# One slot plan for the LayerNorm steps of both attention halves

## The chip, the cores and the metric

The kernel runs on one core of a Trainium2 chip. The metric is device time in microseconds (us) of one execution. Engines are named as in the profile: PE (TensorE matmuls), PEld (its weight loads), DVE (VectorE), ACT (ScalarE), POOL (GpSimd), SP (SyncE, which here only issues DMAs). Every engine takes its instructions in the order in which they stand in its own queue.

## The reference

One transformer block on x of 2048 rows by 512, with modulation by a conditioning vector c. Attention has 32 query heads in groups of 4 per key/value head (8 of these, 128 wide) over the last 512 keys of a cache; the feed-forward network (FFN) is a gated GELU of width 1792.

```python
mod = (_silu(c) @ w_mod).reshape(c.shape[0], 6, 1, -1)
sa, ca, ga, sb, cb, gb = (mod[:, j] for j in range(6))
h = _layernorm(x) * (1 + ca) + sa
q = h @ wq                                   # 32 heads of 128
p = softmax(q @ k^T * Dh ** -0.5)            # k, v: last 512 rows of the caches
x = x + ga * ((p @ v) @ wo)
h = _layernorm(x) * (1 + cb) + sb
x = x + gb * ((gelu(h @ w_gate) * (h @ w_up)) @ w_down)
```

## The kernel before

Matrix products are made of three fp16 matmuls each (`mm3`, lines 86 to 88): every operand is held as a high half and a low half, and high x high, high x low and low x high are added up in PSUM. Rows of x are handled in four blocks of 512 (QB). Attention runs over two halves of the rows, each half two blocks; for each half it goes through 16 pairs of heads, and for each pair through 4 units (one head, one block of 512 rows). A unit is four **slots** of 128 rows. So there are 512 slots, 16 to a pair of heads, and T = 512. In the text the place of a slot is its number modulo 16.

The order of all work is written out by a loop over slots, and no scheduler changes it. In slot t the code issues, in this order:

```python
scores(t)                      # PE: 3 matmuls into ps (2 banks)
peak(t)                        # DVE L906: nm, the negated maximum of a row
if t % 2 == 0: recips(t - 2)   # DVE L925
run(("d", t))                  # what was set down for slot t: q and PV results (L674 ACT, L675 DVE), sums (L694), y (L883)
low(t - 3)                     # DVE L934: the low half of p; then SP's transpose pt<-p (L938)
expo(t)                        # ACT L915: ee = exp(ps - max)
high(t - 2)                    # ACT L929: the high half of p
for _ in range(3): pop()       # PE: 3 groups of 3 matmuls from the queue of work
run(t); run(("w", t))          # transposes that are due; then steps placed "w": weights (POOL), LayerNorm
spare(t)                       # one of the loads and stores that may go out (bg), by their due slots
```

A slot thus has 12 matmuls, 2.59 us when PE never stops; at place 3 the queue of work is empty after 6, and the slot takes 1.3. Since ps has two banks, the scores of slot t + 2 wait until the exponential of slot t has read its bank. On DVE every slot has the maximum and the low half of p. At places 1, 3, 7, 13 and 15 that is all but for an instruction on a column now and then; at the other places there are one to three more instructions over 128x512.

During the first attention half the second half's rows of the first LayerNorm are made (`ln_pair`, gen 1), and during the second half those of the second LayerNorm for the FFN's first half (gen 2). A third run of such work, gen 3, lies under the FFN and has a plan of its own. For each gen there are four chunks (i = 0 to 3), each with two blocks of 128 rows (k = 0 and 1, tiles xs, of which there are two). Its steps are: `load` (SP: xs<-in_x or xs<-y), `stat` (DVE L381, L383, L385, and POOL's power L391), `norm` first (DVE L473: subtract the mean, times a row) and second (DVE L471: times rs, plus a row), `sub` (POOL L479, four differences, for a product with fewer multiplications), and for four sides `high` (ACT L489), `low` (POOL L492) and `turn` (SP L496, a DMA transpose into the tiles B, C, T1, T2 that PE reads).

`plan_pair` places these steps: PLAN has offsets from a base slot b, for block 0 (load, stat, norm first, norm second), for block 1 the same, then the two slots of subtractions, then (high, low, turn) of each side. Loads have due slots from b + l to b + l + 3. With the numbers before, gen 1 has b = 78 + 32 i and gen 2 b = 287 + 48 i.

Beside LayerNorm POOL prepares weights in the first half: scales (kmax, lw, vmax and so on: a power L233, then L237), wq by L160, L156, L157, L729, and wo by L584, L156, L157. DVE takes reciprocals of these scales (kinv L248, wsc L271, lr L263, vsc L648) in its own queue three slots after the scale was set down. In the second half POOL prepares the FFN's weights (stage), which SP stores (kept<-stage).

Of the kernel before, what the change touches and what calls it, by code (L numbers as in the profile page):

```python
# [25 lines left out]
QT = QB // P  # L26
# [37 lines left out]
def block_kernel(ctx: ExitStack, tc: tile.TileContext, x, kT, v, wq, wo, wg, wu, wd, cT, wc, wm, out):  # L64
# [35 lines left out]
    def rows_of(t, i):  # L100
        return t[i * P:(i + 1) * P, :]
# [233 lines left out]
    def within(lo, hi, fn):  # L335
        at(("w", max(lo, 0)), lambda: bg.append((hi, lo, 0, fn)))
# [6 lines left out]
    BK, hs, y1 = {}, {}, {}  # L343
# [113 lines left out]
    def ln_pair(gen, i, src):  # L457
        by, shift = (1, 0) if gen < 2 else (4, 3)
        X, S, st = {}, {}, [{}, {}]

        def load(k):
            X[k] = pool.tile([P, D], F32, tag="ln", name="xs", bufs=2)
            dma(X[k], src(k))

        def stat(k):
            ln_stat(X[k], st[k])
            ln_power(st[k])

        def norm(k, second):
            if second:  # L470
                nc.vector.scalar_tensor_tensor(X[k], X[k], st[k]["rs"], ROWS[shift], op0=ALU.mult, op1=ALU.add)  # L471
            else:
                nc.vector.scalar_tensor_tensor(X[k], X[k], st[k]["mv"][:, 0:1], ROWS[by], op0=ALU.subtract, op1=ALU.mult)  # L473

        def sub(o, a, b):
            def at_(n):
                return X[n // 2][:, n % 2 * 256:n % 2 * 256 + 256]

            nc.gpsimd.tensor_tensor(at_(o), at_(a), at_(b), op=ALU.subtract)  # L479

        def alloc(s):
            S[s] = pool.tile([P, 1 if s == 1 else 2, 2, 256], F16, tag="turn", name="turn", bufs=2)

        def side(s):
            k = (0, 1, 0, 1)[s]
            return X[k][:, 256:512].rearrange("p (h q) -> p h q", h=1) if s == 1 else X[k].rearrange("p (h q) -> p h q", h=2)

        def high(s):
            nc.scalar.activation(S[s][:, :, 0, :], side(s), AF.Copy)  # L489

        def low(s):
            nc.gpsimd.tensor_tensor(S[s][:, :, 1, :], side(s), S[s][:, :, 0, :], op=ALU.subtract)  # L492

        def turn(s):
            moved[0] += 1
            nc.sync.dma_start_transpose(block(gen, ("B", "C", "T1", "T2")[s])[:, i], S[s].rearrange("p a b c -> p (a b c)"))  # L496

        return load, stat, norm, sub, alloc, high, low, turn
# [167 lines left out]
    def at(key, *fns):  # L666
        later.setdefault(key, []).extend(fns)
# [259 lines left out]
    def high(t):  # L927
        p16 = pool.tile([P, 2, W], F16, tag="p16", name="p16", bufs=NP16)
        nc.scalar.activation(p16[:, 0, :], E[t]["e"], AF.Copy, scale=E[t]["r"])  # L929
        E[t]["p16"] = p16  # L930

    def low(t):
        p16 = E[t]["p16"]
        nc.vector.scalar_tensor_tensor(p16[:, 1, :], E[t]["e"], E[t]["r"], p16[:, 0, :], op0=ALU.mult, op1=ALU.subtract)  # L934
        u, i = divmod(t, 4)
        if i == 0:
            pT[u] = pool.tile([P, QT, 2 * KT, P], F16, tag="pt", name="pt", bufs=NPT)
        nc.sync.dma_start_transpose(pT[u][:, i], p16.rearrange("p a b -> p (a b)"))  # L938
        E.pop(t)
# [158 lines left out]
    for p in range(2):  # L1098
        for k, (load, steps) in enumerate(combos(p, nc.gpsimd if p == 0 else nc.vector, 1 if p else 2, 0 if p else 5)):
# [5 lines left out]
            else:  # L1105
                sched(base + steps[0][0], (load, [fn for _, fn in steps]), *[base + off for off, _ in steps[1:]])

    PLAN = {1: (-6, 0, 2, 4, -1, 6, 8, 16, 20, 21, ((8, 9, 12), (18, 19, 22), (24, 25, 28), (28, 29, 33))),
            2: (-6, 0, 2, 5, 8, 14, 16, 18, 21, 22, ((7, 8, 11), (19, 20, 23), (25, 26, 29), (31, 32, 35)))}

    def plan_pair(gen, b, i, src):
        load, stat, norm, sub, alloc, high, low, turn = ln_pair(gen, i, src)
        l0, s0, a0, b0, l1, s1, a1, b1, u, v, sides = PLAN[gen]
        for k, (l, s, x, y) in enumerate(((l0, s0, a0, b0), (l1, s1, a1, b1))):
            within(b + l, b + l + 3, lambda k=k: load(k))
            at(("w", b + s), lambda k=k: stat(k))
            at(("w", b + x), lambda k=k: norm(k, False))
            at(("w", b + y), lambda k=k: norm(k, True))
        for s, (h, l, t) in enumerate(sides):
            at(("w", b + h), lambda s=s: alloc(s), lambda s=s: high(s))  # L1120
            at(("w", b + l), lambda s=s: low(s))
            at(b + t, lambda s=s: turn(s))
        at(("w", b + u), lambda: sub(0, 2, 0), lambda: sub(2, 3, 2))
        at(("w", b + v), lambda: sub(3, 3, 0), lambda: sub(1, 1, 3))
# [3 lines left out]
    for j in (3, 4):  # L1128
        at(257 + 2 * j, lambda j=j: row_make(j))
    for i in range(QT):  # L1130
        plan_pair(1, 78 + 32 * i, i, lambda k, i=i: rows_of(x, 2 * QT + QT * k + i))
        plan_pair(2, 287 + 48 * i, i, lambda k, i=i: y1[QT * k + i])

    def store_set(key, k):
        store(("w", key, k), SET[key][k])
# [294 lines left out]
    with tc.manual_schedule():  # L1430
        begin()
        nexty = []
        for t in range(T + TAIL):
            now[0] = t
            u, s = divmod(t, 4)
# [149 lines left out]
```

## Time and profile before

| | |
|---|---|
| runs | 1762.35, 1762.66, 1764.65 us (median 1762.66) |
| the profiled execution | 1763.88 us, of which 1762.1 is the span from first to last instruction |
| granted PE clock | 0.999 |
| attention, first half | about 25 to 690 us of the span |
| attention, second half | to 1336 us |
| FFN | the rest |
| maximum (L906), alone | 0.68 us a row, 512 of them |
| low half of p (L934), median and longest | 0.74 and 1.78 us, 512 of them |

Rows of single instructions read: start (us from the span's start), duration, engine, line, operation, output<-inputs, shapes, how many; in brackets the idle time of the engine ahead of it and what ended it. A row's start is what counts for the queue, since an instruction's row may end some hundredths after the next one began. Rows of stretches read: the stretch, its length, busy time of each engine with its number of instructions, clock, DMA share, GB/s. Rows of waits read: who waited <- for whom: us in total, times, longest.

### The profile page before, as it was taken

Reading aid. Unit: us, or ns where it says so; the run is one execution under the profiler, and the core shown is the slowest. Engines: PE = TensorE matmul, PEld = TensorE weight load, DVE = VectorE, ACT = ScalarE, POOL = GpSimd, SP = SyncE. Lnnn points to the kernel's source line nnn. Section 1 sums busy time; section 2 is a strip of 40 time slices with the busy share of each in tenths; the row PEclk is TensorE's granted clock in tenths of the full one; section 3 lists DMA queues with packets and bytes.
Section 4 is the critical chain, followed back from the end, with each engine's and each line's share of the span. In section 5 each row is a group of like instructions: output and inputs, shape, how many; then the busy total and the mean of one; then the engine's idle time right before and its main releaser. Section 6 shows DMA issues by size and latency. Waiting matters only on the chain.

```text
span 1762.1 us, 25746 instructions
## 1 busy us (share of the span) xinstructions
PE 1724.3 (98%) x8034; PEld 787.8 (45%) x8034; DVE 1455.9 (83%) x2541; ACT 1207.7 (69%) x2716; POOL 896.2 (51%) x1113
## 2 busy tenths in 40 slices
PE   8899999999999999999999999999999999999999
PEld 5444444444444444444444444444444444444444
DVE  7888898989898889888888897988875788676666
ACT  6888877777777877778878778788774344434333
POOL 4879878887888773216666667666300233000000
PEclk9999999999999999999999999999999999999999
DMA  7999999999998998999999999999976545252222
GB/s 233 215 195 212 207 213 202 220 199 220 209 213 195 225 203 163 204 214 218 220 214 220 233 223 206 227 224 216 201 143 140 168 127 134 81 200 75 87 75 75
DMA packets 691690, 328.14 MB, mean 186 GB/s; under 512 B 596960, under 2 KB 607456, under 8 KB 691552
## 3 DMA queue, kind: packets, MB, share of 16 engines
q1 hardware_dynamic: 691264, 325.97, 81.0%
q8 instruction: 63, 1.03, 0.2%
q14 instruction: 75, 0.61, 0.1%
q10 hardware_dynamic: 288, 0.52, 0.1%
HBM read 127.54 MB, written 53.61 MB: 103 GB/s over the span
## 4 chain that ended last, share of the span: by engine, by line
PE 77%; POOL 8%; DVE 7%; ACT 4%; issue 2%; DMA 1%; SPq 0%; POOLq 0%; ACTq 0%
PE py L88 8%; PE py L86 8%; PE py L87 8%; PE ps L86 5%; PE ps L88 5%; PE ps L87 5%; PE po L86 5%; PE po L88 5%; PE po L87 5%; PE fa L86 3%; PE fa L88 3%; PE fa L87 3%; PE qa L86 2%; PE qa L88 2%; PE qa L87 2%
## 5 line engine op out<-in xcount | busy, mean ns | idle before, releaser
L915 ACT ACTIVATE ee<-ps,nm 128x512 f32<-128x512 f32 x512 | 350.1, 684 | 265.5 <-DVE nm L906 263.6
L934 DVE SCALAR_TENSOR_TENSOR p<-ee,rr,p 128x512 f16<-128x512 f32 x512 | 452.8, 884 | 1.8 <-ACT p L929 1.5
L906 DVE TENSOR_REDUCE nm<-ps 128x1 f32<-128x512 f32 x512 | 349.9, 683 | 97.3 <-PE ps L88 95.1
L929 ACT ACTIVATE p<-ee,rr 128x512 f16<-128x512 f32 x512 | 363.1, 709 | 8.8 <-DMA pt<-p 8.0
L86 PE MATMUL ps<-k,qt 128*128 128x512 f16 x512 | 193.8, 379 | 20.9 <-ACT ee L915 20.2
L86 PE MATMUL po<-pt,v 128*128 128x512 f16 x512 | 194.1, 379 | 1.6 <-DVE p L934 0.8
L88 PE MATMUL ps<-k,qt 128*128 128x512 f16 x512 | 194.1, 379 | 1.3 <-DVE qt L675 1.3
L87 PE MATMUL py<-wo,ot 128*128 128x512 f16 x512 | 194.0, 379 | 0.0
L88 PE MATMUL py<-wo,ot 128*128 128x512 f16 x512 | 194.0, 379 | 0.0
L88 PE MATMUL po<-pt,v 128*128 128x512 f16 x512 | 194.0, 379 | 0.0
L87 PE MATMUL po<-pt,v 128*128 128x512 f16 x512 | 194.0, 379 | 0.0
L86 PE MATMUL py<-wo,ot 128*128 128x512 f16 x512 | 194.0, 379 | 0.0
L87 PE MATMUL ps<-k,qt 128*128 128x512 f16 x512 | 193.9, 379 | 0.0
L391 POOL TENSOR_TENSOR rs<-rs,nhalf 128x1 f32<-128x1 f32 x32 | 23.4, 731 | 227.4 <-DVE rs L385 224.6
L675 DVE SCALAR_TENSOR_TENSOR ot<-po,ot 128x512 f16<-128x512 f32 x128 | 87.0, 680 | 39.5 <-ACT ot L674 39.3
L87 PEld LDWEIGHTS <-w 128*128 128x128 f16 x728 | 71.3, 98 | 87.0 <-issue 1.7
L88 PEld LDWEIGHTS <-w 128*128 128x128 f16 x728 | 71.3, 98 | 86.6 <-issue 0.8
L86 PEld LDWEIGHTS <-w 128*128 128x128 f16 x728 | 71.2, 98 | 86.7 <-DMA w<-kept 1.3
L883 DVE SCALAR_TENSOR_TENSOR acc<-py,ysc,acc 128x512 f32<-128x512 f32 x128 | 94.5, 738 | 10.9 <-PE py L88 10.9
L883 DVE SCALAR_TENSOR_TENSOR acc<-py,dysc,acc 128x512 f32<-128x512 f32 x112 | 81.3, 744 | 26.4 <-PE py L88 26.2
L915 ACT ACTIVATION_READ_ACCUMULATOR ee<-ps,nm 128x1 f32 x512 | 99.4, 194 | 0.0
L86 PE MATMUL py<-wo,at 128*128 128x512 f16 x224 | 84.9, 379 | 0.0
(269 smaller groups left out, 3760.6 us busy)
## 6 DMA issues: line engine op xcount, KB each, us to landing
w<-kept SPq DMA_DIRECT2D x123, 256.0 KB, 3.3
wo<-kept SPq DMA_DIRECT2D x60, 256.0 KB, 3.5
raw<-in_wo SPq DMA_DIRECT2D x56, 256.0 KB, 3.1
kept<-stage SPq DMA_DIRECT2D x56, 256.0 KB, 3.1
kept<-w SPq DMA_DIRECT2D x39, 256.0 KB, 3.2
rw<-in_wq SPq DMA_DIRECT2D x38, 256.0 KB, 3.2
pt<-p SPq DMA_TRANSPOSE x512, 3.4
kept<-wo SPq DMA_DIRECT2D x32, 256.0 KB, 2.7
```

The lines of the kernel that those rows point to most:

```text
L86: nc.tensor.matmul(ps, lhi, rhi, start=first, stop=False, skip_group_check=chain)
L87: nc.tensor.matmul(ps, lhi, rlo, start=False, stop=False, skip_group_check=chain)
L88: nc.tensor.matmul(ps, llo, rhi, start=False, stop=last, skip_group_check=chain)
L391: nc.gpsimd.tensor_tensor(st["rs"], st["rs"], nhalf, op=ALU.pow)
L675: return lambda: nc.vector.scalar_tensor_tensor(t[:, 1, :], src, scale, t[:, 0, :], op0=ALU.mult, op1=ALU.subtract)
L883: nc.vector.scalar_tensor_tensor(acc[ti], st["p"], by, acc[ti], op0=ALU.mult, op1=ALU.add)
L906: nc.vector.tensor_reduce(nm, E[t]["ps"], axis=AX.X, op=ALU.max, negate=True)
L915: nc.scalar.activation(e, E[t]["ps"], AF.Exp, bias=E[t]["nm"], scale=1.0, accum_out=sm[:, t % 2:t % 2 + 1])
L929: nc.scalar.activation(p16[:, 0, :], E[t]["e"], AF.Copy, scale=E[t]["r"])
L934: nc.vector.scalar_tensor_tensor(p16[:, 1, :], E[t]["e"], E[t]["r"], p16[:, 0, :], op0=ALU.mult, op1=ALU.subtract)
```

## The change

The two plans become one, and the bases move: gen 1 from 78 to 77 + 32 i, gen 2 from 287 to 285 + 48 i (both are place 13 of 16 with the new base).

```diff
-    PLAN = {1: (-6, 0, 2, 4, -1, 6, 8, 16, 20, 21, ((8, 9, 12), (18, 19, 22), (24, 25, 28), (28, 29, 33))),
-            2: (-6, 0, 2, 5, 8, 14, 16, 18, 21, 22, ((7, 8, 11), (19, 20, 23), (25, 26, 29), (31, 32, 35)))}
+    PLAN = (-6, 0, 2, 4, 0, 6, 10, 16, 19, 20, ((7, 8, 12), (17, 18, 22), (23, 24, 28), (27, 28, 32)))
...
-        l0, s0, a0, b0, l1, s1, a1, b1, u, v, sides = PLAN[gen]
+        l0, s0, a0, b0, l1, s1, a1, b1, u, v, sides = PLAN
...
-        plan_pair(1, 78 + 32 * i, i, lambda k, i=i: rows_of(x, 2 * QT + QT * k + i))
-        plan_pair(2, 287 + 48 * i, i, lambda k, i=i: y1[QT * k + i])
+        plan_pair(1, 77 + 32 * i, i, lambda k, i=i: rows_of(x, 2 * QT + QT * k + i))
+        plan_pair(2, 285 + 48 * i, i, lambda k, i=i: y1[QT * k + i])
```

As slots (chunk i = 0; the place modulo 16 in brackets):

| step | gen 1 before | gen 1 after | gen 2 before | gen 2 after |
|---|---|---|---|---|
| statistic, block 0 | 78 (14) | 77 (13) | 287 (15) | 285 (13) |
| norm first, block 0 | 80 (0) | 79 (15) | 289 (1) | 287 (15) |
| norm second, block 0 | 82 (2) | 81 (1) | 292 (4) | 289 (1) |
| load due, block 1 | 77 to 80 | 77 to 80 | 295 to 298 | 285 to 288 |
| statistic, block 1 | 84 (4) | 83 (3) | 301 (13) | 291 (3) |
| norm first, block 1 | 86 (6) | 87 (7) | 303 (15) | 295 (7) |
| norm second, block 1 | 94 (14) | 93 (13) | 305 (1) | 301 (13) |
| subtractions | 98, 99 | 96, 97 | 308, 309 | 304, 305 |
| high halves (ACT) | 86, 96, 102, 106 | 84, 94, 100, 104 | 294, 306, 312, 318 | 292, 302, 308, 312 |
| low halves (POOL) | 87, 97, 103, 107 | 85, 95, 101, 105 | 295, 307, 313, 319 | 293, 303, 309, 313 |
| transposes (SP) | 90, 100, 106, 111 | 89, 99, 105, 109 | 298, 310, 316, 322 | 297, 307, 313, 317 |

On DVE, the queue around slots 86 and 87 (gen 1, i = 0; nm is the maximum, p the low half, xs the LayerNorm tile, row the modulation row, qt and ot results of PE, acc the sum of y). Before:

```order
L906 TENSOR_REDUCE nm<-ps 128x1
L925 RECIPROCAL rr<-rr 128x2
L675 SCALAR_TENSOR_TENSOR qt<-qd,qsc,qt 128x512
L883 SCALAR_TENSOR_TENSOR acc<-py,ysc,acc 128x512
L934 SCALAR_TENSOR_TENSOR p_3158<-ee,rr,p_3158 128x512
L473 SCALAR_TENSOR_TENSOR xs<-xs,mv,row 128x512
L906 TENSOR_REDUCE nm<-ps 128x1
L934 SCALAR_TENSOR_TENSOR p_3186<-ee,rr,p_3186 128x512
L231 TENSOR_REDUCE ysc<-pst 128x1
```

The same place after the change:

```order
L906 TENSOR_REDUCE nm<-ps 128x1
L925 RECIPROCAL rr<-rr 128x2
L675 SCALAR_TENSOR_TENSOR qt<-qd,qsc,qt 128x512
L883 SCALAR_TENSOR_TENSOR acc<-py,ysc,acc 128x512
L934 SCALAR_TENSOR_TENSOR p_3160<-ee,rr,p_3160 128x512
L906 TENSOR_REDUCE nm<-ps 128x1
L934 SCALAR_TENSOR_TENSOR p_3189<-ee,rr,p_3189 128x512
L473 SCALAR_TENSOR_TENSOR xs<-xs,mv,row 128x512
L231 TENSOR_REDUCE ysc<-pst 128x1
```

The first norm step of block 1 went from the end of slot 86 to the end of slot 87.

On DVE, slots 82 to 84 (places 2 to 4) before:

```order
L883 SCALAR_TENSOR_TENSOR acc<-py,ysc,acc 128x512
L934 SCALAR_TENSOR_TENSOR p_3025<-ee,rr,p_3025 128x512
L471 SCALAR_TENSOR_TENSOR xs<-xs,rs,row 128x512
L906 TENSOR_REDUCE nm<-ps 128x1
L934 SCALAR_TENSOR_TENSOR p_3060<-ee,rr,p_3060 128x512
L906 TENSOR_REDUCE nm<-ps 128x1
L925 RECIPROCAL rr<-rr 128x2
L675 SCALAR_TENSOR_TENSOR ot<-po,ot 128x512
L934 SCALAR_TENSOR_TENSOR p_3092<-ee,rr,p_3092 128x512
L381 BN_STATS bn<-xs 128x6
```

and after:

```order
L883 SCALAR_TENSOR_TENSOR acc<-py,ysc,acc 128x512
L934 SCALAR_TENSOR_TENSOR p_3025<-ee,rr,p_3025 128x512
L906 TENSOR_REDUCE nm<-ps 128x1
L934 SCALAR_TENSOR_TENSOR p_3061<-ee,rr,p_3061 128x512
L381 BN_STATS bn<-xs 128x6
L383 BN_AGGR mv<-bn 128x2
L385 TENSOR_SCALAR rs<-mv 128x1
L906 TENSOR_REDUCE nm<-ps 128x1
L925 RECIPROCAL rr<-rr 128x2
L675 SCALAR_TENSOR_TENSOR ot<-po,ot 128x512
```

The second norm step of block 0 left slot 82, and the statistic of block 1 went from slot 84 into the short slot 83.

On POOL, slots 95 to 98 of chunk 0 (turn is a low half, xs<-xs the subtractions, lw to ksc the scales of the next pair's weights, rw the weights themselves) before:

```order
L233 TENSOR_TENSOR lw<-lw,half__86 128x1
L237 TENSOR_SCALAR lw<-lw 128x1
L237 TENSOR_SCALAR lu<-lw,kmax,ma 128x1
L259 TENSOR_TENSOR lt<-lu,half__86 128x1
L237 TENSOR_SCALAR lt<-lt 128x1
L492 TENSOR_TENSOR turn<-xs,turn 128x256
L237 TENSOR_SCALAR qsc<-lt 128x1
L237 TENSOR_SCALAR lr<-lr,lu 128x1
L237 TENSOR_SCALAR ksc<-lr,kinv 128x1
L479 TENSOR_TENSOR xs<-xs 128x256 x2
L160 TENSOR_SCALAR rw<-rw,wsc 128x512
```

and after:

```order
L492 TENSOR_TENSOR turn<-xs,turn 128x256
L233 TENSOR_TENSOR lw<-lw,half__86 128x1
L237 TENSOR_SCALAR lw<-lw 128x1
L237 TENSOR_SCALAR lu<-lw,kmax,ma 128x1
L259 TENSOR_TENSOR lt<-lu,half__86 128x1
L237 TENSOR_SCALAR lt<-lt 128x1
L479 TENSOR_TENSOR xs<-xs 128x256 x4
L237 TENSOR_SCALAR qsc<-lt 128x1
L237 TENSOR_SCALAR lr<-lr,lu 128x1
L237 TENSOR_SCALAR ksc<-lr,kinv 128x1
L160 TENSOR_SCALAR rw<-rw,wsc 128x512
```

The low half now stands ahead of the power of lw, and all four subtractions ahead of qsc, lr and ksc; before, two of them stood behind ksc and two behind the first piece of wq.

## The prediction

> **What bounds the kernel now.** I read the busy shares first, then who waited for whom on TensorE (PE) by stage, then busy time per stretch of 32 slots, and last the single rows around the stops.
>
> ```profile
> PE 1724.3 (98%) x8034; PEld 787.8 (45%) x8034; DVE 1455.9 (83%) x2541; ACT 1207.7 (69%) x2716; POOL 896.2 (51%) x1113
> ```
> ```profile
> core 0: us, PE busy (x) PEld busy (x) DVE busy (x) ACT busy (x) POOL busy (x), PEclk, DMA share, GB/s
> 571.70:652.48 80.78, 80.53 (x377) 36.44 (x376) 67.76 (x122) 63.15 (x151) 60.01 (x75) 1.00 1.00 217
> 139.75:221.04 81.29, 81.29 (x387) 37.45 (x386) 70.16 (x123) 65.56 (x156) 70.55 (x88) 1.00 0.98 210
> 252.69:337.56 84.87, 81.23 (x378) 36.46 (x378) 74.33 (x133) 65.68 (x159) 69.23 (x88) 1.00 0.94 210
> ...
> 422.38:507.20 84.82, 81.23 (x377) 36.48 (x377) 74.31 (x133) 65.69 (x159) 69.19 (x88) 1.00 0.93 209
> 507.20:591.15 83.95, 81.06 (x378) 36.29 (x377) 71.18 (x127) 67.19 (x163) 67.39 (x90) 1.00 0.93 208
> ```
> PE is the bound, at full clock, so only its stops can be won. Each stretch above is 32 slots. The first two lie before and after the LayerNorm (LN) work of the first attention half and run without a stop (one of 0.4 us in the first): 81 us. The next three (first and last shown; the middle one also takes 84.82) carry one chunk of LN each and take 84.8 with the same matmuls. Two views of waits, PE from 228 to 570 us, then from 570 to 1340 us:
>
> ```profile
> PE ps L86 <- ACT ee L915: 13.9, 15, 1.9
> PE ps L88 <- DVE qt L675: 1.0, 1, 1.0
> PE qa L86 <- ACT u L816: 0.4, 1, 0.4
> ...
> PE po L86 <- DVE p L934: 0.8, 1, 0.8
> PE ps L86 <- ACT ee L915: 0.3, 1, 0.3
> ```
> So first-half LN costs at most about 18.6 us: 15.3 us in 17 stops; 2.7 because each stop is 0.16 longer than it shows (a matmul's row lasts 0.38 us, while the next may start 0.22 after it); and some 0.6 in gaps too small for this view. In the second half there is next to nothing to win, and the third group of LN, under the FFN, is not touched. These are the stops of one chunk in order of time, then two of the last chunk:
>
> ```profile
> 252.69 0.38 PE L86 MATMUL ps<-k,qt 128*128 128x512 f16 x1 [1.63 <-ACT ee L915]
> 293.54 0.38 PE L86 MATMUL ps<-k,qt 128*128 128x512 f16 x1 [0.49 <-ACT ee L915]
> 321.27 0.38 PE L86 MATMUL ps<-k,qt 128*128 128x512 f16 x1 [0.17 <-ACT ee L915]
> 325.08 0.38 PE L86 MATMUL ps<-k,qt 128*128 128x512 f16 x1 [1.06 <-ACT ee L915]
> 337.56 0.38 PE L86 MATMUL ps<-k,qt 128*128 128x512 f16 x1 [1.91 <-ACT ee L915]
> ...
> 538.65 0.38 PE L86 MATMUL ps<-k,qt 128*128 128x512 f16 x1 [0.85 <-ACT ee L915]
> 550.93 0.38 PE L86 MATMUL ps<-k,qt 128*128 128x512 f16 x1 [0.62 <-ACT ee L915]
> ```
> All wait for the exponential (L915), which waits for the maximum (L906), which stands in VectorE's (DVE's) queue behind LN. The first of them, in rows of DVE and PE (slots 85 to 87):
>
> ```profile
> 242.79 0.69 DVE L381 BATCH_NORM_STATS2 bn<-xs 128x6 f32<-128x512 f32 x1
> 243.80 0.68 DVE L906 TENSOR_REDUCE nm<-ps 128x1 f32<-128x512 f32 x1
> 245.69 0.38 PE L86 MATMUL ps<-k,qt 128*128 128x512 f16 x1
> 245.69 0.68 DVE L906 TENSOR_REDUCE nm<-ps 128x1 f32<-128x512 f32 x1
> ...
> 248.08 1.58 DVE L934 SCALAR_TENSOR_TENSOR p<-ee,rr,p 128x512 f16<-128x512 f32 x1
> 249.59 1.64 DVE L473 SCALAR_TENSOR_TENSOR xs<-xs,mv,row 128x512 f32<-128x512 f32 x1
> 251.15 0.68 DVE L906 TENSOR_REDUCE nm<-ps 128x1 f32<-128x512 f32 x1
> ```
> Slot 86's DVE work runs from 245.69 to 251.15, 5.46 us against a slot of 2.59, because the second block's first norm step (L473) stands there behind maximum, two low halves and an accumulation. Slot 87's scores began at 245.69 and their maximum at 251.15. I call that lateness: 5.46. Scores two slots on need the same bank, so they start 1.54 us after that maximum (252.69). The stop was 1.63 + 0.16 = 1.79, so a lateness of 5.46 - 1.79 = 3.67 would have been free. Where one of the two slots is the short one (place 3 of 16, 1.3 us), about 2.35 is free.
>
> **The change, part by part.** Nothing is added or removed; six DVE steps per chunk move, and with them ACT casts, POOL work and transposes. A statistic costs DVE 243.80 - 242.79 = 1.01 us. A norm step (first row; the second norm step, L471, reads alike) costs
>
> ```profile
> L473 DVE SCALAR_TENSOR_TENSOR xs<-xs,mv,row x24: 736/745/1647, 231.7 to 1489.2; 128x512 f32<-128x512 f32 x24
> L381 DVE BATCH_NORM_STATS2 bn<-xs x24: 679/686/695, 226.5 to 1486.0; 128x6 f32<-128x512 f32 x24
> ```
> 0.67 us when alone, since an instruction starts about 0.07 before the row ahead of it ends, and 1.56 (249.59 to 251.15) when POOL works beside it.
>
> *First norm step of block two, place 6 to place 7.* Slot 86 then takes 3.9 us at most (245.69 to 249.59). Its start also comes earlier. Before, its maximum began when the scores of slot 87 did, one slot (2.6) late. The statistic at 242.79 now stands before the maximum of slot 84, in the room of the norm step that left slot 82; so its 1.0 us leaves slot 84, with a 0.5 wait there for a cast that now comes sooner, and lateness at 86 falls to about 1.0. Slot 87 starts at 1.0 + 3.9 - 3.0 = 1.9. It holds only maximum and low half:
>
> ```profile
> 319.64 0.38 PE L86 MATMUL ps<-k,qt 128*128 128x512 f16 x1
> 321.96 1.65 DVE L471 SCALAR_TENSOR_TENSOR xs<-xs,rs,row 128x512 f32<-128x512 f32 x1
> 323.54 0.68 DVE L906 TENSOR_REDUCE nm<-ps 128x1 f32<-128x512 f32 x1
> ...
> 324.80 0.68 DVE L906 TENSOR_REDUCE nm<-ps 128x1 f32<-128x512 f32 x1
> ```
> 1.26 us (323.54 to 324.80). With the norm at 0.67 to 1.56, and up to 0.9 more if the low half meets POOL too, slot 88 starts at 1.9 + 1.26 + 1.56 + 0.0..0.9 - 2.6 = 2.1 to 3.0, under 3.67. The stop goes in all four chunks: 1.79 + 3 x 2.07 = **8.0 us**.
>
> *Second norm step of block one, place 2 to place 1.* It is the 1.58 us (321.96 to 323.54) ahead of slot 115's maximum, which began 3.90 after its scores (319.64) and so stopped slot 117 for 1.22, after 0.33 at slot 116. Without it lateness is 3.90 - 1.58 = 2.32, at the free 2.35, and the wait for kmax below goes as well. In its place slot 113 gets 0.67 to 1.56, which that light slot's spare 2.59 - 1.26 = 1.33 nearly takes. I count all three chunks, 3 x 1.55 = **4.7 us**; the low end is half of it.
>
> *POOL: low halves and subtractions earlier.* DVE waits of 228 to 570 us, and POOL rows of chunk one:
>
> ```profile
> DVE vsc L648 <- POOL lw L237: 11.9, 4, 3.1
> ...
> DVE kinv L248 <- POOL kmax L237: 3.1, 3, 1.0
> ```
> ```profile
> 271.86 0.57 POOL L233 TENSOR_TENSOR lw<-lw,half__86 128x1 f32<-128x1 f32 x1 [2.69 <-DVE lw L183]
> 275.28 1.02 POOL L492 TENSOR_TENSOR turn<-xs,turn 128x256 f16<-128x256 f32 x1 [0.67 <-ACT turn L489]
> 277.85 0.27 POOL L237 TENSOR_SCALAR lr<-lr,lu 128x1 f32<-128x1 f32 x1 [1.38 <-DVE lr L263]
> ```
> The reciprocal vsc holds DVE for 3.0 us a chunk since POOL comes to its power late; that makes the stop at 293.54. The low half of 1.02 now stands ahead of the 2.69 gap and the four subtractions ahead of the 1.38 gap, while the work before vsc's power stays the same. So POOL arrives 1.02 + 0.67 + 1.38 = 3.1 us sooner, which covers 3.0: 3 x 0.65 = **1.9 us**, and **0.5** of 0.17 us stops behind kmax. In the last chunk POOL already has no gap (four pieces of wo stand together ahead of it), so its 3.5 us (529 to 551) stay, and the low half put ahead of the power costs about **-0.5**.
>
> *Statistic of block two on the short slot.* It may run into its load, which keeps its slots:
>
> ```profile
> 315.71 0.74 DVE L934 SCALAR_TENSOR_TENSOR p<-ee,rr,p 128x512 f16<-128x512 f32 x1
> ...
> 319.66 0.48 SPq L94 DMA_DIRECT2D xs<-in_x x1
> ...
> DMA to landing us min/median/max: 2.6/3.7/4.8
> ```
> The load leaves 3.95 us after the low half ahead of it (slot 112) begins, and lands 7.7 to 8.8 after that. That low half begins about 1.34 after its maximum, and slot 115's statistic 1.26 after its own; with three slots between, the statistic is due 7.77 - 1.34 + 1.26 = 7.7 later, and up to 8.9 if lateness grows by 1.2 on the way. So DVE waits 0 to 1.1 us, and behind it POOL's power (L391) with the wq work queued there. Lateness at slot 116 becomes 2.7 to 3.5, still free: 0, with an end of -0.5 per chunk.
>
> *ACT casts* go to places 4, 14, 4, 8, where ACT has only exponential and high half: 0, hidden by PE. *Transposes* stand four slots behind their low half instead of three: 0 in the first half. *Second half:* LN stands in places 13, 15, 1 and 4 there and stops PE for 0.3 us at most, and the new places are no heavier; the other stop (0.8 + 0.16, for p) may go or come again elsewhere: 0, ends +1 and -2.
>
> The rule that speaks against the change is the Trainium skill's: "SBUF — State Buffer", section on the two separate sides, says that VectorE with two SBUF inputs and GpSimd take a shared port pair as an exclusive lock for a whole instruction. The rows agree in kind: 745 to 1647 ns for the norm step, and 679 to 695 for the one-input statistic. Read strictly, moving steps leaves the locked total, and the time, as they are; that is the second rival.
>
> Sum: 8.0 + 4.7 + 1.9 + 0.5 - 0.5 = 14.6 us. The profiled execution took 1763.88 us around a span of 1762.1, the median of the runs 1762.66. 1763.88 - 14.6 = 1749.3 for a profile, **1748.1** for the median.
>
> **Rivals.** *Half is won (0.17).* The norm step at place 7 still meets POOL and both low halves are slow, lateness passes 3.67 by some tenths, and the statistic waits for its load. Then the second-block stops keep about 0.7 each (2.8), half of 4.7 stays, and 0.5 per chunk comes from the load: 14.6 - 2.8 - 2.4 - 2 = 7.4, so 1755. For it speaks my margin of 0.6 us; against it the earlier start of every slot.
>
> *Nothing is won (0.07).* DVE and POOL do the same work on the same ports in the same period, so the stops only move: 1762. Against it: 139.75 to 221.04 holds as much POOL work (70.55) without a stop, and DVE's 74.33 of 81 us are spans that overlap by a tenth.
>
> *Slower (0.06).* SP issues in order, and the load of block two stands behind three stores. If DVE waited 4 us for it, past the 1.0 us of lateness left at slot 116, each of eight chunks would stop 3 us, and 1748.1 + 24 = 1772. From a wait of 14.6 / 8 + 1.0 = 2.8 us it decides; the slowest landing seen is 4.8, 1.1 over the median, and my count has 1.1 at the most.
>
> **How the numbers follow.** Forecast 0.70, at 1748.1, its own range 1744 (all 18.6) to 1752; rivals 0.17, 0.07, 0.06. The range to 1755.5 takes in most of the half-won case and leaves out about 0.17. A difference of 0.2% (3.5 us) is about what can be told from none. Faster: 0.70 + 0.17 = 0.87; same 0.07; slower 0.06.
>
> **What would show it.** In the profile after: stretches of 32 slots in the first half at 80.4 to 81.5 us; PE's wait for L915 between 228 and 570 us down from 13.9 to under 4, what is left around slots 193 to 201; DVE's wait for vsc three times shorter than 0.5. Wrong would be new waits of L381 for the xs load, or PE's wait for L915 moved to places 5 and 10 of 16.

## The result, and the profile after

The changed kernel takes 1753.44 us (median of six runs, 1750.25 to 1754.06) against 1762.52 for the kernel before, measured beside it: 9.1 us less, a ratio of 0.9943 with an interval of 0.993 to 0.9956. The profiled execution took 1753.77 us around a span of 1751.9, 10.1 us less than the one before. So it is faster by 0.6%; 14.6 us had been forecast.

The four stretches that hold a chunk of LayerNorm (LN) in the first half, each from the start of slot 89, 121, 153 and 185 to that of the 32nd slot on, now read so:

```profile
core 0: us, PE busy (x) PEld busy (x) DVE busy (x) ACT busy (x) POOL busy (x), PEclk, DMA share, GB/s
251.48:331.89 80.41, 80.41 (x378) 36.48 (x377) 74.96 (x133) 66.53 (x159) 70.56 (x88) 1.00 1.05 220
...
492.72:577.36 84.64, 81.43 (x378) 36.15 (x377) 71.81 (x125) 66.06 (x160) 67.02 (x90) 1.00 0.96 205
```

The first three take 80.4 us each (the second and third read like the first), with PE busy all the time; only the last keeps stops. DVE, ACT and POOL are about as busy as before: their work was not made less, it stands where nobody waits for it. PE's waits from 228 to 560 us are few, and all of them lie in the last chunk:

```profile
PE ps L88 <- DVE qt L675: 1.1, 2, 0.8
PE ps L86 <- ACT ee L915: 1.0, 2, 0.6
PE po L88 <- POOL v L157: 0.8, 1, 0.8
PE qa L88 <- POOL w L157: 0.3, 1, 0.3
```

PE's wait for the exponential (L915) was 13.9 us there. DVE's wait for vsc, 11.9 us in four before, is one wait, in the last chunk:

```profile
DVE vsc L648 <- POOL lw L237: 2.3, 1, 2.3
```

Where the time comes from and goes is seen best if the start of each slot's scores is compared between the two traces (before minus after, so positive is earlier):

| slot | 0 | 77 | 121 | 153 | 185 | 205 | 285 | 301 | 305 | 396 | 400 | 416 | end |
|---|---|---|---|---|---|---|---|---|---|---|---|---|---|
| lead, us | 0.1 | -0.6 | 5.7 | 10.1 | 14.5 | 13.8 | 13.5 | 13.5 | 9.6 | 9.8 | 8.7 | 9.7 | 10.1 |

From slot 77 to 205 the first half wins 14.4 us. Ahead of slot 77 the code is the same, and 0.6 was lost. Then 3.9 us go at slots 302 to 304, in the second half. There PE waits for a transposed p:

```profile
796.60 0.38 PE L86 MATMUL po<-pt,v 128*128 128x512 f16 x1 [2.30 <-issue]
796.82 0.38 PE L87 MATMUL po<-pt,v 128*128 128x512 f16 x1
...
798.48 0.64 PE L87 MATMUL po<-pt,v 128*128 128x512 f16 x1
798.90 0.64 PE L88 MATMUL po<-pt,v 128*128 128x512 f16 x1
```

The stop is 2.30 + 0.16 us. About 1 us after it the matmuls start 0.42 us apart instead of 0.22 (798.48 to 798.90 against 796.60 to 796.82), which costs some 1.7 us more. That makes 4.2; the kernel before loses 0.25 in the same slots, which leaves 3.9. "issue" here hides a DMA: SP's queue shows the transpose of p that PE waits for, issued at 792.76; in the trace it lands 3.75 us later, at 796.51.

```profile
781.75 1.23 SPq L938 DMA_TRANSPOSE pt<-p  x1
786.18 0.34 SPq L94 DMA_DIRECT2D rw<-in_wu  x1
786.57 0.42 SPq L94 DMA_DIRECT2D kept<-stage  x1
787.09 2.90 SPq L938 DMA_TRANSPOSE pt<-p  x1
790.04 1.32 SPq L496 DMA_TRANSPOSE B<-turn  x1
791.45 0.53 SPq L94 DMA_DIRECT2D rw<-in_wu  x1
792.03 0.62 SPq L94 DMA_DIRECT2D kept<-stage  x1
792.76 1.27 SPq L938 DMA_TRANSPOSE pt<-p  x1
```

SP gets behind because the load of rw had to wait (781.75 + 1.23 to 786.18), by SP's waits (from 772 to 802 us) for POOL, which prepares the FFN's weights (stage):

```profile
SPq L94 <- POOL stage L157: 3.1, 1, 3.1
```

And LN's own transpose (B<-turn, L496) now stands in this crowded stretch ahead of the late p. With the plan of before it stood behind that p.

### The profile page after: what moved, and what is told of

It reads as the page before. It is cut to its first block, busy times and chain, and to the rows that moved or that the text cites. A ratio compares the mean times of both kernels' runs of the same rounds, so it can differ in the third digit from the quotient of the medians.

```text
span 1751.9 us, 25755 instructions
## 1 busy us (share of the span) xinstructions
PE 1722.1 (98%) x8034; PEld 787.2 (45%) x8034; DVE 1460.0 (83%) x2541; ACT 1211.5 (69%) x2716; POOL 899.0 (51%) x1113
## 4 chain that ended last, share of the span: by engine, by line
PE 89%; POOL 4%; DVE 3%; issue 1%; ACT 1%; DMA 1%; SPq 0%; POOLq 0%; ACTq 0%
PE py L88 9%; PE py L87 9%; PE py L86 9%; PE ps L86 6%; PE po L86 6%; PE po L88 6%; PE po L87 6%; PE ps L88 6%; PE ps L87 6%; PE fa L86 3%; PE fa L88 3%; PE fa L87 3%; PE qa L87 3%; PE qa L86 3%; PE qa L88 3%
## 5 line engine op out<-in xcount | busy, mean ns | idle before, releaser
L915 ACT ACTIVATE ee<-ps,nm 128x512 f32<-128x512 f32 x512 | 350.4, 684 | 250.5 <-DVE nm L906 247.8
L915 ACT ACTIVATION_READ_ACCUMULATOR ee<-ps,nm 128x1 f32 x512 | 99.3, 194 | 0.0
L492 POOL TENSOR_TENSOR turn<-xs,turn 128x512 f16<-128x512 f32 (+1 forms) x48 | 55.8, 1164 | 69.5 <-ACT turn L489 69.2
```

The source lines that it names most:

```text
L915: nc.scalar.activation(e, E[t]["ps"], AF.Exp, bias=E[t]["nm"], scale=1.0, accum_out=sm[:, t % 2:t % 2 + 1])
```

## Experiments

Each time is a median, and the difference is to the kernel before as run beside it on the same chip (1762.52 us for the changed kernel, else 1762.98, 1762.81 or 1763.38).

| kernel | us | to before |
|---|---|---|
| changed kernel | 1753.44 | -9.1 |
| new plan in the first half only | 1748.20 | -14.8 |
| new plan in the second half only | 1766.50 | +3.5 |
| second half: first transpose one slot later | 1748.83 | -14.2 |
| same, and its low half two slots later (**base** below) | 1747.59 | -15.4 |
| base, first norm step of block two back | 1747.30 | -15.5 |
| base, statistic of block two back | 1746.76 | -16.1 |
| base, both of these back | 1747.72 | -15.7 |
| base, both back, and POOL's first low half with its transpose | 1747.47 | -15.9 |
| base, second norm step of block one back | 1748.94 | -13.9 |
| base, POOL's low halves and subtractions back | 1760.78 | -2.0 |
| same, and their transposes back | 1757.78 | -5.6 |
| base, last chunk's later steps 16 slots later | 1744.07 | -19.3 |

### Which half won, which lost

The two plans were separated again, each half with its own base. First the new plan for the first half alone:

```diff
-    PLAN = (-6, 0, 2, 4, 0, 6, 10, 16, 19, 20, ((7, 8, 12), (17, 18, 22), (23, 24, 28), (27, 28, 32)))
+    PLAN = {1: (-6, 0, 2, 4, 0, 6, 10, 16, 19, 20, ((7, 8, 12), (17, 18, 22), (23, 24, 28), (27, 28, 32))),
+            2: (-6, 0, 2, 5, 8, 14, 16, 18, 21, 22, ((7, 8, 11), (19, 20, 23), (25, 26, 29), (31, 32, 35)))}
-        plan_pair(2, 285 + 48 * i, ...
+        plan_pair(2, 287 + 48 * i, ...
```

> First half with the new plan and base, second half with the old plan and base 287. Theory A (the first half gained the 14.4 us forecast, the second half's new plan gives back about 4 at slots 302 and 398): 1748 to 1750 us, no stop at slots 302 to 305 over 0.5 us, the 1.0 us stop at slot 414 back. Rival B (the loss after slot 301 comes with the new phase of the first half or from run to run, not from the second half's plan): 1752 to 1754.

It took 1748.2 us (1747.71 to 1748.68). Then the other way round, the old plan and base for gen 1 and the new ones for gen 2:

> First half with the old plan and base 78, second half with the new plan and base 285. Theory A: slower than before by 3 to 4 us, 1765.5 to 1766.5, with the stop of over 2 us at slot 302. Rival B: 1762 to 1763, no such stop.

It took 1766.5 us, slower than before (ratio 1.0018, 1.0009 to 1.0027). PE's waits from 750 to 1330 us, of the first kernel and then of the second:

```profile
PE po L86 <- DVE p L934: 0.6, 1, 0.6
PE po L86 <- DMA pt<-p: 0.2, 1, 0.2
```
```profile
PE po L86 <- issue: 2.3, 1, 2.3
PE po L86 <- DMA pt<-p: 1.1, 1, 1.1
```

The stop of 2.3 us comes with the second half's new plan, whatever the first half does, and without it the forecast of 1748.1 is met within 0.1 us. The theory holds; the rival (run to run, or the first half's phase) falls.

### What in the second half lost it

Only gen 2's first transpose moves here, one slot later (297 to 298), so that SP again issues it behind the next p:

```diff
-            2: (... ((7, 8, 12), (17, 18, 22), ...
+            2: (... ((7, 8, 13), (17, 18, 22), ...
```

> As after, but in the second half the transpose of the first side one slot later (slot 298 + 48 i for 297 + 48 i), which puts SP's row B<-turn behind one more transpose of p, as before the change. Theory A1 (SP's queue: the B<-turn row ahead of the transposes of p makes them late): the stops at slots 302 to 305 go, 1749.5 to 1750.5. Rival A2 (POOL: the low half ahead of the FFN weights' pieces holds the load on SP until its tile is free): stop at 302 stays, 1753 to 1754.

The time was 1748.83 us, 5.1 less than with the changed kernel by the differences to before (4.6 by the times). SP's queue at the same place:

```profile
785.45 0.34 SPq L94 DMA_DIRECT2D rw<-in_wu  x1
785.84 0.42 SPq L94 DMA_DIRECT2D kept<-stage  x1
786.35 1.48 SPq L938 DMA_TRANSPOSE pt<-p  x1
787.92 1.46 SPq L94 DMA_DIRECT2D rw<-in_wu  x1
789.43 0.62 SPq L94 DMA_DIRECT2D kept<-stage  x1
790.16 1.29 SPq L938 DMA_TRANSPOSE pt<-p  x1
791.50 1.53 SPq L496 DMA_TRANSPOSE B<-turn  x1
```

From the load of rw to the p that PE waits for it is now 790.16 - 785.45 = 4.71 us, and was 792.76 - 786.18 = 6.58. Of the 1.87 us between, the moved transpose itself is 1.4 (790.04 to 791.45). PE's stop there falls from 2.30 to 0.60, and the slow matmuls behind it don't come.

In the next kernel the low half on POOL goes back as well, to slot 295, behind the pieces of FFN weights for which SP's load waits:

```diff
-            2: (... ((7, 8, 13), (17, 18, 22), ...
+            2: (... ((7, 10, 13), (17, 18, 22), ...
```

> As the kernel with the transpose of the first side one slot later, and the first side's low half on POOL two slots later too (slot 295 + 48 i), as before the change. Theory A1: as that kernel, 1749.5 to 1750.5, within 0.7 us of it. Rival A2: only here the stops at slots 302 to 305 go, and it is 3 us faster than that kernel.

1747.59 us, 1.2 less, with 0.05 us of the stop at slot 302 left. SP's wait for POOL's stage is 2.3 us now, as in the kernel before, and was 3.1. So both theories have a share: in this order the row of SP took 4.6 to 5.1 us (with the slow matmuls) and the low half 1.2. The low half was not put back alone, so what it would have been worth by itself is not shown.

### What in the first half won it

All that follows is set against this last kernel (the base), of which gen 1's plan is changed. First the step to which the prediction gave most, the first norm step of block two, back from place 7 to place 6:

```diff
-    PLAN = {1: (-6, 0, 2, 4, 0, 6, 10, 16, ...
+    PLAN = {1: (-6, 0, 2, 4, 0, 6, 9, 16, ...
```

> Base for this and the next three is the kernel with the second half's first low half and transpose later (1747.6 us). Here block two's first norm step in the first half goes back from place 7 to place 6 (offset 10 to 9), nothing else. Theory P (the prediction's first term: the norm step's place pays 8.0 us): stops of 1.8 to 2.1 us at slots 89, 121, 153 and 185, 1755.6 us. Rival Q (it pays mostly because the statistic left slot 84; with it in the short slot 83, slot 86 starts only 1.3 late, slot 87's maximum then at 1.3 + 5.46 - 2.59 = 4.2, 0.5 over the free 3.67): stops of about 0.5, four times 0.5 to 0.7, 1749.6 to 1750.5.

1747.30 us: nothing came back, neither P's stops nor Q's. Next the statistic (offset 6 to 7), with the norm step at place 7:

> Block two's statistic in the first half back from place 3 to place 4 (slot 84 + 32 i), the norm step stays at place 7. Theory P: the lateness at slot 88 goes from 1.5 to 2.5 to 3.0, still free, 1747.3 to 1748.5 us. Rival Q: stops of 1 to 2 us come back at slots 89, 121, 153 and 185, 1752 to 1755.

1746.76 us, no stop either. As neither step alone brought one, both were put back (6, 10 to 7, 9):

> In the first half block two's statistic back at place 4 and its first norm step back at place 6, both. Theory T (either alone sufficed; the stop at slot 89 also needed block one's norm at slot 82 and POOL beside the low half of p): lateness at slot 87 about 1.8 + 4.6 - 2.6 = 3.8, stops of 0 to 0.3, 1747.3 to 1748.6 us. Rival P (these two are the whole first term): stops near 1.8 four times, 1755.

1747.72 us, no stop. And with POOL's first low half and its transpose in their slots of before, too ((7, 8, 12) to (7, 10, 13)):

> As the kernel with the statistic and the first norm step back, and POOL's first low half back at slot 87 with its transpose at 90, plus 32 i. Theory T: the low half of p in slot 86 meets POOL again (1.6 us for 0.74), lateness at slot 87 about 1.8 + 5.46 - 2.59 = 4.7, stops of about 1.0 four times, 1751.3 to 1752.5 us. Without that meeting 1747.3 to 1748.8.

1747.47 us, and still no stop at slots 89, 121, 153 and 185. Its rows (slots 86 and 87) show how near that was:

```profile
244.82 0.38 PE L86 MATMUL ps<-k,qt 128*128 128x512 f16 x1
...
246.19 0.74 DVE L934 SCALAR_TENSOR_TENSOR p<-ee,rr,p 128x512 f16<-128x512 f32 x1
246.85 1.65 DVE L473 SCALAR_TENSOR_TENSOR xs<-xs,mv,row 128x512 f32<-128x512 f32 x1
248.42 0.68 DVE L906 TENSOR_REDUCE nm<-ps 128x1 f32<-128x512 f32 x1
```

The norm step stands ahead of slot 87's maximum as before the change, and takes 1.6 us. But the maximum is 248.42 - 244.82 = 3.60 us late instead of 5.46, just under the free 3.67. Three things make the 1.86: DVE comes to slot 86 1.79 late instead of 2.59, since the other norm step has left slot 82; a wait of 0.2 for qt is gone; and the low half of p takes 0.66 to the next start instead of 1.51. POOL does the same work at that moment as before the change, in the other order of starts. Its rows of the kernel before, then of this one:

```profile
247.96 1.16 POOL L157 TENSOR_TENSOR w<-rw,w 128x512 f16<-128x512 f32 x1
```
```profile
246.29 1.66 POOL L157 TENSOR_TENSOR w<-rw,w 128x512 f16<-128x512 f32 x1
```

Before, POOL's piece of w began 0.12 ahead of that p (247.96 against 248.08) and p took 1.58; here it begins 0.10 behind it (246.29 against 246.19), p takes 0.74 and POOL 1.66. It is so in all four chunks. The piece that p met was not LN's low half (L492), which began only at 249.08, 1.0 after that p. So the expectation that p would be slow beside POOL again failed by the order of two starts, a tenth of a microsecond each way; with 3.60 against a free 3.67, that no stop came is luck in part.

The second norm step of block one, from place 1 back to place 2 (offset 4 to 5):

> Block one's second norm step in the first half back from place 1 to place 2 (offset 4 to 5). Theory P (second term, 4.7 us): stops of 1.2 at slots 117, 149 and 181, 1752.3 us. Rival R (POOL's new order takes the wait for kmax away, and with it 1.0 of that lateness): stops under 0.5, 1748 to 1749.5.

1748.94 us, 1.4 more than the base, near the rival. The stops at slots 117, 149 and 181 don't come back; all of it is one stop at slot 196 of the last chunk, 1.94 us where the base has 0.57. The step is felt all the same: DVE comes to slot 86 2.4 us late where the base has 1.1, still short of a stop. The mechanism of the rival was not tested by itself.

### POOL's steps, and what hangs on them

The low halves and subtractions alone, in the slots of before:

```diff
-    PLAN = {1: (... 16, 19, 20, ((7, 8, 12), (17, 18, 22), (23, 24, 28), (27, 28, 32))),
+    PLAN = {1: (... 16, 21, 22, ((7, 10, 12), (17, 20, 22), (23, 26, 28), (27, 30, 32))),
```

> In the first half POOL's low halves and subtractions back to the slots of before (87, 97, 103, 107 and 98, 99, plus 32 i); DVE and ACT keep the new places. Theory P (third term, 2.4 us less 0.5): DVE waits about 3 us for vsc three times, stops of 0.5 at slots 105, 137 and 169, 1749.5 to 1750.2 us. Rival S (the wait comes back but is covered, since slot 102 now starts less late): 1747.3 to 1748.2.

Neither: 1760.78 us, 13.2 more. PE's waits from 228 to 570 us:

```profile
PE po L86 <- DVE kmax L181: 5.3, 2, 2.6
PE ps L86 <- ACT ee L915: 3.2, 7, 0.9
PE po L86 <- DVE bn L381: 2.1, 1, 2.1
```

PE's product with pt (po) stops at slots 110, 142 and 174, for 2.1, 2.6 and 2.6 us, the last two with slow matmuls behind them; kmax and bn are only what DVE finished last, and what came late is the transposed p. LN's transposes stood two slots behind their low halves, and in SP's queue one of them stands ahead of a late p (at 301.57, with transposes of p at 299.59 and 303.63), as in the second half. So the next kernel puts them back, too:

```diff
+    PLAN = {1: (... 16, 21, 22, ((7, 10, 13), (17, 20, 23), (23, 26, 29), (27, 30, 34))),
```

> POOL's low halves and subtractions of the first half in the slots of before, and SP's transposes too (90, 100, 106, 111 plus 32 i), so that each stands behind its low half by as many slots as before. Theory SP (the 13 us lost with the low halves alone moved back came from transposes two slots behind their low halves, where SP waits for POOL and holds the transposes of p): no stops at slots 110, 142 and 174; 1749.2 to 1750.5, the 0.6 us stops at 105, 137 and 169 stay. Rival N (the loss comes from POOL's order itself): 1757 to 1761.

1757.78 us: the stops at 110, 142 and 174 fall to 0.4, 0.9 and 1.0, but 10.2 us over the base stay, and the rival is right that most of the loss comes from POOL's order. The trace says how. DVE's waits from 228 to 570 us:

```profile
DVE vsc L648 <- POOL lw L237: 10.1, 4, 2.5
...
DVE bn L381 <- DMA xs<-in_x: 6.1, 4, 2.8
```

The wait for vsc is back at slots 102, 134 and 166. It stops PE at 105, 137 and 169, 0.6 us each, as the prediction had it. DVE stays late behind it: slot 108's maximum begins 3.6 us after its scores, as in the kernel before (3.6), against 1.3 in the changed one. And SP is held by POOL, too. SP's waits for LN's low half from 228 to 570 us, of this kernel and then of the kernel before, and three rows of SP in this kernel:

```profile
SPq L94 <- POOL turn L492: 12.5, 3, 4.2
```
```profile
SPq L94 <- POOL turn L492: 6.0, 4, 1.9
```
```profile
291.64 1.23 SPq L938 DMA_TRANSPOSE pt<-p  x1
297.12 0.33 SPq L94 DMA_DIRECT2D xs<-in_x  x1
297.55 1.23 SPq L938 DMA_TRANSPOSE pt<-p  x1
```

The next chunk's first load (xs<-in_x) waits until POOL is through with the third low half of this chunk, which reads the old xs: 4.2 us in each of three chunks, here and in the kernel above. In the kernel before, where that load is due one slot later, the wait is 1.9 at most; in the changed kernel there is none. The transposes of p stand behind that load: the four p that DVE finishes from 293.8 to 302.5 us leave 2.8 to 3.7 us after that. Rows of PE and DVE around slot 109, where the next chunk's first statistic stands:

```profile
301.44 0.38 PE L86 MATMUL ps<-k,qt 128*128 128x512 f16 x1
...
304.43 1.70 DVE L934 SCALAR_TENSOR_TENSOR p<-ee,rr,p 128x512 f16<-128x512 f32 x1
...
305.73 0.38 PE L86 MATMUL po<-pt,v 128*128 128x512 f16 x1 [0.41 <-DMA pt<-p]
306.05 0.68 DVE L906 TENSOR_REDUCE nm<-ps 128x1 f32<-128x512 f32 x1
```

Slot 109's maximum is 306.05 - 301.44 = 4.6 us late (1.5 in the changed kernel, where the scores stand at 302.0), and the low half of p ahead of it takes 1.70, beside a piece of wo and a low half of LN on POOL. So p comes late as well, and SP does not catch up before the load of block two. That load leaves 18.3 us after the scores of slot 109 in this kernel and 13.9 after them in the changed one:

```profile
319.77 0.47 SPq L94 DMA_DIRECT2D xs<-in_x  x1
...
323.96 0.69 DVE L381 BATCH_NORM_STATS2 bn<-xs 128x6 f32<-128x512 f32 x1 [1.47 <-DMA xs<-in_x]
...
326.53 0.38 PE L86 MATMUL ps<-k,qt 128*128 128x512 f16 x1 [0.74 <-ACT ee L915]
```
```profile
315.85 0.47 SPq L94 DMA_DIRECT2D xs<-in_x  x1
```

The statistic on the short slot waits for it, 1.5, 1.6 and 2.8 us in three chunks, and PE stops at slots 118, 150 and 182 for 0.7 to 1.1. That is the slower rival of the prediction, the load late behind SP's queue. Against the base, by starts of matmuls, the stops of slots 110 to 182 cost 8.0 us (3.5 around slots 110, 142 and 174, 1.1 at slot 113 for qa, 3.4 for the load of block two), those of vsc 1.8. That this loss begins with the wait of the first load is read from the trace; no kernel moved that load alone.

### A faster version

In the last chunk POOL has four pieces of wo ahead of the second low half. Here the second, third and fourth side and the subtractions go 16 slots later, behind these pieces:

```diff
+            3: (-6, 0, 2, 4, 0, 6, 10, 16, 35, 36, ((7, 8, 12), (33, 34, 38), (39, 40, 44), (43, 44, 48)))}
-        ... = PLAN[gen]
+        ... = PLAN[3 if gen == 1 and i == 3 else gen]
```

> Base is the kernel with the second half's first low half and transpose later (1747.6 us). In the first half's last chunk, the second, third and fourth sides (high, low, transpose) and the subtractions go 16 slots later, to slots 206 to 221, behind the four pieces of wo on POOL. Theory L (the 4.0 us of stops at slots 196 to 202 come from POOL being behind there): they fall to under 1 us in all, 1743.8 to 1745.0 us. Rival M (the stops move with the steps to slots 208 to 218, since POOL has the next pair's weights there): 1746.5 to 1748.

1744.07 us (1743.04 to 1744.48; ratio to before 0.9891, 0.9877 to 0.9904), 3.5 less than the base (3.9 by the differences to before). PE's waits from 478 to 560 us:

```profile
PE ps L86 <- ACT ee L915: 0.4, 1, 0.4
PE ps L88 <- DVE qt L675: 0.2, 1, 0.2
```

The stops at slots 198 to 202 are gone, and none comes up to slot 228, so they did not move with the steps. This version beats both kernels.

## Why the prediction was right in part

- **The sum of the first half** was right: 14.4 us from slot 77 to 205 where 14.6 stood, and 1748.2 with the new plan there alone. The stretches of 80.4 us, the wait for L915 at 1.0, the rest around slots 196 to 202 are as it said, and the rival in which nothing is won falls. It is right as a sum of stops, for nearly all of them went; which step removes which stop it had mostly wrong.
- **First norm step of block two, 8.0 us.** The stops went, but not because of that step: it can be put back, with the statistic and a low half, at no cost. A stop is what exceeds a free limit, here 5.46 - 3.67 = 1.8 us. The change takes 4.0 off the lateness at slot 87 (5.45 to 1.45): 1.6 for the norm step, 1.3 for the earlier start, 0.8 for p that doesn't meet POOL, 0.4 for the wait for qt. The prediction named the earlier start but put the whole price on the one step. The others were enough without it; the norm step's 1.6 alone would have been 0.2 short by these numbers, and was not tried. One sum is wrong, too: 1.0 + 3.9 - 3.0 = 1.9 takes off 3.0 for a slot of 2.6. With 2.6, slot 88 would start 2.5 to 3.4 late, with little room under 3.67; that it measured 1.5 made up for it.
- **Second norm step of block one, 4.7 us.** Also over-covered: alone it is worth 1.4 us, in the last chunk, which the sum had left out, and nothing in the three that it counted. That its leaving slot 82 takes 0.8 off the lateness four slots on had no price in the sum.
- **POOL order, 1.9 + 0.5.** The direct part was right to its size (three stops of 0.6 come back without it). What was mis-sized is all that hangs on it: with POOL late, DVE stays late from slot 102 on, and SP's next load of xs waits 4.2 us for a low half and holds the transposes of p; that and the load of block two behind it take 8.0 us more. So some 10 of the first half's 14 us hang on this term, once the bases and statistics stand where the change put them. Beside it stands the line on the short slot, of which the prediction said that the load "keeps its slots" and DVE waits at most 1.1 us: that holds (no such wait over 0.2 in the changed kernel) only as long as SP is in time.
- **Last chunk, 3.5 us stay and -0.5:** 4.2 us of stops at slots 196 to 202, right.
- **Second half, "0, ends +1 and -2".** This is the step that failed, and most of the 5.5 us by which the result missed the forecast: -3.9 at slots 302 to 304. "The new places are no heavier" was read from DVE alone. On SP the moved transpose costs 1.4 us of a queue that was already late, and POOL's low half ahead of the weights makes SP's load wait 0.8 longer (3.1 against 2.3). The end of -2 did not hold what a stop of over 2 us brings after it, 1.7 us of slow matmuls. The wait for p at slot 414 went, and one of 1.0 at slot 398 came, as the prediction allowed.
- **The range.** 1753.44 lies outside the forecast's own range of 1744 to 1752. It lies under 1755.5 because the range took in the rival in which half is won, and that rival's reasons (stops kept behind the norm step, a statistic that waits for its load) did not occur. That it covers the result is luck.
- The rest is small: -0.6 ahead of slot 77 in identical code, -0.3 from 205 to 285, +0.5 from there to the end.

What stays open: why the transpose at 787.09 took 2.90 us, and which step brings the stop at slot 89 back. With the whole old plan of the first half (the kernel with the new plan in the second half only) it is there, 1.63 us; with three steps back it is not, and nothing between these two was tried.

## What to carry to other kernels

A stop that several moves each remove is not a sum of their prices: write down the excess over the free limit and what each move takes off it, and expect the first sufficient one to be worth all and the others nothing. When a step moves, follow its DMA, too, and what stands behind its row in an in-order queue of DMA issues; and when a load moves earlier, ask whether the tile that it fills is free by then. Two places with the same room on the busiest engine are not the same on the queue beside it.

## What the hardware showed unasked

A stop of PE of about 2 us can halve its clock for a while. Behind the 2.30 us stop the granted clock over the slow matmuls reads 0.54:

```profile
797.70:801.40 3.70, 3.70 (x11) 1.39 (x10) 0.88 (x2) 1.25 (x4) 0.67 (x1) 0.54 1.13 230
```

In the profiles of this case, from about 60 us on, stops of 1.8 to 1.94 us were never followed by it; those of 2.30 to 2.65 always were (four), and one of 2.09 was not. At slot 28, in the start-up that all 14 kernels share, the stop is 1.98 to 2.02 us, and slow matmuls followed in 9 of 14. Where they didn't, slot 29 starts some 1.6 us earlier, but PE then stops in it for p, 0.7 to 1.1 us, so that 0.3 to 0.8 us are left. That is a part of how the start-up differs between executions of the same code. The Trainium skill, "TensorE: Matmul & The Clock Gate", part 1, says that the clock falls to half after an idle window of about 3.4 us, that such windows run freely, and that it takes one busy window to come back. The stretch at half clock here, some 3.5 us, and the chance at slot 28 agree with a free-running window; but stops of 2.0 to 2.65 us were enough, well under 3.4, and there the measurement decides.
